# Exact block of ones for the bonus from the sixth unit on, and v weight conversions and two preparations issued behind masks and states

## Chip, cores and metric

The kernel runs on one core of a Trainium2 chip, as one program. The metric is the device time of one execution in microseconds (us). TensorE (PE; its weight loads are listed as PEld), VectorE (DVE), ScalarE (ACT), GpSimd (POOL) and SyncE (SP) work beside each other; each takes its instructions in the order in which they stand in the program, and waits for another engine or for a transfer by semaphores. SP issues most transfers, ACT some.

## The reference, cut to what matters

Three layers follow each other: a linear attention with a decaying state, a gated feed-forward layer, and a gated layer that mixes over the sequence.

```
B, H, S, D = 2, 8, 768, 48
for t in range(S):
    cur = einsum('bhd,bhe->bhde', u * k[t], v[t])
    y[t] = einsum('bhd,bhde->bhe', r[t], state + cur)
    state = w[t][..., None] * state + einsum('bhd,bhe->bhde', k[t], v[t])
...
xk = mu_k * x + (1 - mu_k) * x_prev;  xr = mu_r * x + (1 - mu_r) * x_prev
k = maximum(xk @ w_k, 0);  v = (k * k) @ w_v;  r = sigmoid(xr @ w_r);  x = r * v
...
h = gelu(x @ w_in);  u, v = split(h);  v = norm(v) * g
x = x + (u * (w_sg @ v + b_sg)) @ w_out
```

The term with `u` is the bonus: `y[t]` gets `v[t]` times the sum over d of `r[t] * u * k[t]`, a number for each token and head. The inputs are f32.

## The kernel before

The tokens are cut into four groups of 384 (two batches by two halves). The attention of one group is done for four pairs of heads, so there are 16 units of work, numbered here from 0 as in the code: unit g is head pair g % 4 of group g // 4. Each unit holds three chunks of 128 tokens. Units 0 to 3 run at the start, where little else is there to do. From then on the three matrix products of the first feed-forward layer of one group (keys "k", "r", "v") fill TensorE while the four units of the next group are put in between them. Units 4 to 7 thus stand among the feed-forward steps of group 0. The order of TensorE's instructions is written out by hand (`plan`, a list of keys with estimated times, and the loop over `keys` from L1068 on). The order of DVE, ACT, POOL and SP comes from a scheduler with a priority for each instruction (`with at(t)`) and with explicit "issue this behind that" constraints (`tc.issue_after`).

A unit has these steps:

- Preparation, `attn_prep` (L444), on DVE: a running product of the decay (`pf`), its reciprocal, a reversed scan (`pr`), then the scaled `kp` and `rp`. `prep(i)` issues all of it for unit i and first the loads of unit i + 1; `scans(i)` and `products(i)` issue it in two halves.
- `rk_make` (L477), on POOL: `ru`, the product of r and k for the bonus. It is issued behind the first DVE instruction on the scores of the unit before.
- "S", `attn_sc` (L482): on PE the transposes of `kp` (tile `kt_ps`), then what the bonus needs, then the scores `sc`; on DVE the two masked score blocks `am` (L546).
- "K", `attn_kv` (L553): on PE the states `kv`; on DVE the sums `zt`, on ACT the scaled blocks `sblk`.
- "Y", `attn_y` (L603), and "Z", `attn_z` (L618): the output `y` on PE from masked scores, bonus and states (`scar`, `sblk`), its copy to `yo`, and transfers from `yo` to `xx`, the input of the feed-forward layer.

The bonus has two forms. Below `U_DIAG` it is: three products of `ru` with a two-column matrix on PE (L495), then `vb` on DVE (L528), the values scaled by these sums, and six products of `vb` with the identity on PE (L615). From unit `U_DIAG` on (`wide(i)`) it is: `ru` times u is split into two halves by ACT (`rh`, L535) and DVE (`rh`, L537), two products with a block of ones `hblk` on PE give `ab` (L509, L510), and DVE multiplies `ab` with the transposed values `uvt` (L517), which SP loads for these units alone. DVE, not ACT, then adds the result to `y` (L636). `ab` and the `kv` of the same unit lie in one PSUM buffer, so that DVE must have read `ab` before PE can write `kv`. POOL's `ru` of the unit after is issued behind L517.

The weights come as raw 64-bit words. `load64` (L302) issues the load on SP and converts on ACT (`top`, L327) and DVE (L329), by way of two `top` buffers in turn. `conv_moe1` (L379) does this for the 8 blocks of `w_k`, 3 of `w_r`, 8 of `w_v`. The conversions of `w_v` (`wv`) have priorities that put them around units 5 and 6.

Of the kernel before, what the change touches and what calls it, by code (L numbers as in the profile page):

```python
# [24 lines left out]
NP = H // 2  # L25
# [25 lines left out]
T_GAP = 2.5  # L51
T_TAIL = 9.0
VQ = 4
U_DIAG = 6
L_SPLIT = 2
L_CV = 12
L_CVV = 8
L_CK = 6
# [14 lines left out]
def emit(tc, tin, nin, vt, consts, ucp, pars, b_sg, w_k, w_v, w_r, w_in, w_sgT, w_out, outT):  # L73
# [46 lines left out]
    split_ops = [True]  # L120
# [120 lines left out]
    def wide(i):  # L241
        return i >= U_DIAG

# [3 lines left out]
    def load_uvt(i):  # L247
        src = tin[subs[i // NP][0] * NP + i % NP]
        for q in rows(i == U_DIAG):
            with at(TS["Y", i] - (20 if i == U_DIAG else 9)):  # L250
                SP.dma_start(uvts[q], src[q, WL + 2 * G:WL + 3 * G])

    def load_t(i):
# [8 lines left out]
        for q in rows(i < 3):  # L262
            with at(TS["S", min(i, NP - 1)] - 8.5 if 2 <= i <= NP else TS["S", i] - L_UN + 0.5 if i > NP else -19.8 + 0.1 * i), after_table(i in (0,)):
                e.dma_start(rk[q], src[q, WL:WL + 2 * G].rearrange("p (q t) -> p q t", q=2))
        if i == U_DIAG:
            load_uvt(i)
# [17 lines left out]
    wt = {}  # L284
# [14 lines left out]
    def klpair(dt):  # L299
        return pl["w"].tile([128, 2 * WT + 2], dt, name="kl", tag="kl", bufs=KF // 2)  # L300

    def load64(full, src, dl, lc=L_CV):  # L302

        ld = dl - 7
        n_ = early["n"]
        if n_ < N_EARLY:
            stg = pair()
        elif N_EARLY + B_STG <= n_ < N_EARLY + B_STG + KF // 2:
            stg = klpair(U32)
        else:  # L310
            stg = pl["s"].tile([128, 2 * WT + 2], U32, name="stg", tag="stg", bufs=B_STG)
        if n_ < N_EARLY + B_STG + KF // 2:
            ld = T_EARLY + n_ * D_EARLY
        early["n"] += 1
        with at(ld):
            SP.dma_start(stg.bitcast(U16)[:, 1:1 + 4 * WT], src.bitcast(U16))
        n = full.shape[1]

        def box(x):
            return x.rearrange("p (c f) -> p c f", c=n)  # L320

        mid = box(stg[:, 1:1 + 2 * WT].rearrange("p (f w) -> p f w", w=2)[:, :, 0])
        end = box(stg.bitcast(BF16)[:, 4:4 + 4 * WT].rearrange("p (f w) -> p f w", w=4)[:, :, 0])
        top = tops["t"][tops["n"] % B_TOP]
        tops["n"] += 1
        with at(dl - lc - 1):
            A.activation(box(top.bitcast(F16).rearrange("p (f w) -> p f w", w=2)[:, :, 1]), end, AF.Copy)  # L327
        with at(dl - lc):
            V.scalar_tensor_tensor(full.bitcast(U32), mid, 13, box(top), ALU.logical_shift_right, ALU.bitwise_or)  # L329
# [18 lines left out]
    def split_lo(n, behind_):  # L348
        with tc.issue_after(behind_):
            for f in lows[:n]:  # L350
                f()
        del lows[:n]
# [26 lines left out]
    def conv_moe1(first=0, last=2 * KF + KM):  # L379
        def one(nm, i, src, dl):  # L380
            full1(nm, i, [128, KM, 128] if nm != "v" else [128, 1, DM])
            load64(wt[nm, i][0], src[i], dl, {"k": L_CK, "r": L_CV, "v": L_CVV}[nm])
            if NAT[nm] == 0 or (nm == "v" and i >= NVN):
                split1(nm, i, dl - (3 if nm == "v" else 0))

        todo = [("k", f, w_k, TS["k", 0, f]) for f in range(KF)]
        todo += [("r", f, w_r, TS["r", 0, f]) for f in range(KM)]
        todo += [("v", f, w_v, TS["v", 0, 0] + MM[0, "v"] * f) for f in range(KF)]
        for x in todo[first:last]:
            one(*x)  # L390
# [49 lines left out]
    st = {}  # L440
# [584 lines left out]
    def prep(i):  # L1025
        if i < NU:
            if i + 1 < NU and i >= 1:
                load_unit(i + 1)
            for _ in attn_prep(i):
                pass  # L1030
# [37 lines left out]
    for n, key in enumerate(keys[:n_in]):  # L1068
        kd, g = key[0], key[1]
# [50 lines left out]
        if kd == "K":  # L1120
            for f in head.pop("kl", []):
                with tc.issue_after(st[g + 1]["last"][1] if g + 1 in st else st[g]["zt"]), tc.issue_after(st[g]["sb"]):
                    f()
        if kd == "K" and g == 2 * NP - 2:
            with tc.issue_after(st[g]["zt"]), tc.issue_after(st[g]["sa"]):
                for f in range(LO_EARLY):
                    split1("k", f, TS["k", 1, f] - 12, V)
# [4 lines left out]
        if kd == "Z" and g == 2 * NP - 2:  # L1132
            scans(2 * NP)
        elif kd == "Z" and g == 2 * NP - 1:
            with tc.issue_after(st[g]["ev"]):
                products(2 * NP)
                scans(2 * NP + 1)
        elif kd == "Z" and g == 3 * NP - 1:
            with tc.issue_after(st[g]["zt"]):
                scans(g + 1)  # L1140
                products(g + 1)
                scans(g + 2)
        elif kd == "Z" and g == 3 * NP - 2:
            pass
        elif kd == "Z" and NP <= g < 2 * NP:
            prep(g + 2)
        elif kd == "Z" and g >= NP and g + 2 < NU:
            with tc.issue_after(st[g]["zt"]):
                scans(g + 2)
        if kd == "Z" and g >= NP:  # L1150
            if g % NP == NP - 1:
                if g // NP == 1:
# [5 lines left out]
                    a, v = mr[1]()  # L1158
# [5 lines left out]
        if kd == "S":  # L1164
            head["unit"] = g
            if g == LO_LAST:
                split_lo(NVN, st[g]["am"])
            if "sq" in head:
                with behind():
                    head.pop("sq")()  # L1170
# [92 lines left out]
```

## Time and profile before

| | |
|---|---|
| time, median of 3 runs | 335.16 us (335.05 to 335.48) |
| profiled execution, own time | 335.18 us |
| its span, first to last instruction | 333.3 us |
| granted TensorE clock, mean | 0.998 of full speed |
| PE busy | 325.5 us (98%) |
| DVE busy | 239.5 us (72%) |
| ACT busy | 187.1 us (56%) |
| POOL busy | 37.3 us (11%) |
| DVE busy in 45 to 56 us, 66 to 77 us | 9.26, 9.81 us of 11 |

The own time is 1.9 us over the span, what lies around the first and the last instruction. A busy share is taken over the whole span; what an engine has free in one stretch, such as the two in the last row, is read from that stretch. Matmul ends are modelled, so starts of PE instructions are the better guide.

### The profile page before, as it was taken

To read this page: it belongs to the slowest core of one execution; us is meant where nothing else is said; L and a number is where in the kernel's file an instruction comes from. 1 tells how busy PE (TensorE), PEld (TensorE's weight loads), DVE (VectorE), ACT (ScalarE), POOL (GpSimd) and SP (SyncE) were. 2 spreads that over 40 slices of the span, in tenths; PEclk is the share of its full clock that TensorE was granted. 3 is DMA by queue.
4 is the path that set the end of the run, shared out by engine and by line. 5 is a ranking of instruction groups with operands and counts; after the bars stand their busy time and mean duration, and the time that the engine had idled before them with its cause. 6 is when DMAs were issued, how large, how long until landed. Compare 5 with 4: busy or idle time off the path is not lost.

```text
span 333.3 us, 5954 instructions
## 1 busy us (share of the span) xinstructions
PE 325.5 (98%) x2139; PEld 286.2 (86%) x2139; DVE 239.5 (72%) x537; ACT 187.1 (56%) x447; POOL 37.3 (11%) x60
## 2 busy tenths in 40 slices
PE   7999999999999999999999999999999999999993
PEld 3786666666898999999999998998999999999993
DVE  5987998699699995998368451796989724555531
ACT  3566986759688645976369964954533215211100
POOL 3211102010111102011032540000000000000000
PEclk9999999999999999999999999999999999999999
DMA  8879963753524424011036126314140010100022
GB/s 216 213 236 314 289 211 99 207 118 104 177 81 107 111 74 121 16 39 36 24 109 185 53 71 211 94 41 97 49 98 7 1 71 2 63 10 0 0 76 79
DMA packets 23878, 34.22 MB, mean 103 GB/s; under 512 B 3440, under 2 KB 18160, under 8 KB 23840
## 3 DMA queue, kind: packets, MB, share of 16 engines
q1 hardware_dynamic: 21696, 31.34, 32.6%
q10 hardware_dynamic: 2144, 2.41, 2.8%
q8 instruction: 19, 0.31, 0.4%
q14 instruction: 19, 0.16, 0.2%
HBM read 29.02 MB, written 2.36 MB: 94 GB/s over the span
## 4 chain that ended last, share of the span: by engine, by line
PE 90%; ACT 3%; DMA 3%; DVE 1%; issue 1%; SPq 1%; ACTq 0%; DVEq 0%
PE mm L673 46%; PE mn L673 28%; PE sc L514 4%; PE y L612 3%; PE y L626 3%; PE kv L566 2%; DMA cst<-consts 2%; DMA wh<-w_r 1%; PE kt_ps L490 1%; ACT top L327 1%; PE y L615 1%; PE mm L495 1%; ACT sblk L592 1%; DVE pf L458 1%; PE ab L509 1%
## 5 line engine op out<-in xcount | busy, mean ns | idle before, releaser
L661 ACT ACTIVATE gah<-gt 128x384 fp32r<-128x384 f32 x16 | 8.4, 526 | 43.3 <-DVE gt L871 43.3
L480 POOL TENSOR_TENSOR ru<-urk 112x384 f32<-112x384 f32 x15 | 17.3, 1155 | 107.3 <-DVE ru L517 76.6
L592 ACT ACTIVATE sblk<-zt,pf 48x48 f32<-48x48 f32 x62 | 20.5, 330 | 7.6 <-DVE zt L576 4.2
L673 PE MATMUL mm<-kh,wh 128*128 128x384 f32 x64 | 22.0, 344 | 0.0
L673 PE MATMUL mm<-kh,wvl 128*128 128x384 f32 x64 | 21.6, 337 | 0.0
L673 PE MATMUL mm<-kl,wh 128*128 128x384 f32 x64 | 21.5, 337 | 0.0
L673 PE MATMUL mm<-xkh,wh 128*128 128x384 f32 x57 | 20.6, 361 | 0.0
L673 PE MATMUL mn<-wsh,vl 128*128 128x384 f32 x60 | 20.0, 334 | 0.0
L673 PE MATMUL mn<-wsh,vh 128*128 128x384 f32 x60 | 20.0, 334 | 0.0
L673 PE MATMUL mn<-wsl,vh 128*128 128x384 f32 x60 | 20.0, 334 | 0.0
L673 PE MATMUL mm<-xkl,wh 128*128 128x384 f32 x57 | 19.3, 338 | 0.0
L673 PE MATMUL mm<-xkh,wkl 128*128 128x384 f32 x57 | 19.2, 337 | 0.0
L776 DVE TENSOR_TENSOR kl<-kr,kh 128x384 fp32r<-128x384 f32 x24 | 14.1, 600 | 5.5 <-ACT kr L775 5.4
L458 DVE TENSOR_TENSOR_SCAN pf<-uw,d1f 112x387 f32<-112x387 f32 x16 | 16.0, 1005 | 2.4 <-DMA uw<-tin 2.4
L546 DVE TENSOR_TENSOR am<-sc,cst 128x384 f32<-128x384 f32 x32 | 16.1, 545 | 1.3 <-PE sc L514 1.3
L673 PE MATMUL mm<-xkh,wk 128*128 128x384 f32 x48 | 17.0, 497 | 0.0
L334 POOL TENSOR_TENSOR w2l<-wf,w2h 128x384 fp32r<-128x384 f32 x12 | 13.0, 1095 | 35.3 <-ACT w2h L333 35.3
L673 PE MATMUL mm<-kh,wv 128*128 128x384 f32 x48 | 16.3, 490 | 0.0
L327 ACT ACTIVATE top<-stg 128x384 f16<-128x384 bf16 x17 | 10.9, 642 | 8.4 <-DMA stg<-w_in 3.1
L463 DVE TENSOR_TENSOR_SCAN pr<-uw,d1r 112x387 f32<-112x387 f32 x16 | 15.3, 959 | 0.2
L707 ACT ACTIVATE dx<-xx,par 128x384 f32<-128x384 f32 x22 | 12.9, 607 | 4.1 <-DMA xx<-yo 4.0
L514 PE MATMUL sc<-rp,kp 48*128 48x128 f32 x192 | 15.0, 289 | 0.0
(223 smaller groups left out, 976.2 us busy)
## 6 DMA issues: line engine op xcount, KB each, us to landing
urk<-tin SPq DMA_DIRECT2D x26, 144.0 KB, 2.9
wh<-w_k SPq DMA_DIRECT2D x8, 384.0 KB, 5.4
stg<-w_in SPq DMA_DIRECT2D x8, 384.0 KB, 3.6
wq<-tin SPq DMA_DIRECT2D x16, 168.0 KB, 2.4
wsf<-w_sgT SPq DMA_DIRECT2D x12, 192.0 KB, 4.4
outT<-ot SPq DMA_DIRECT2D x12, 192.0 KB, 1.9
uv<-nin ACTq DMA_DIRECT2D x14, 144.0 KB, 3.3
uw<-tin SPq DMA_DIRECT2D x26, 72.8 KB, 2.6
```

The source lines that it names most:

```text
L327: A.activation(box(top.bitcast(F16).rearrange("p (f w) -> p f w", w=2)[:, :, 1]), end, AF.Copy)
L334: e.tensor_tensor(lo, full, hi.bitcast(F32), ALU.subtract)
L458: V.tensor_tensor_scan(pf[:, 0:n1], w[:, 0:n1], d1f[:, 0:n1], 1.0, ALU.mult, ALU.max)
L463: V.tensor_tensor_scan(pr[:, 1:wl][:, ::-1], w[:, 1:wl][:, ::-1], dr[:, 1:wl][:, ::-1], 0.0, ALU.mult, ALU.add)
L480: return e.tensor_tensor(rks[i], urk[i][:, 0], urk[i][:, 1], ALU.mult).ins
L514: PE.matmul(sc[h][:, c], s["kp"][hs, c], s["rp"][hs, c], start=True, stop=True)
L546: s["am"] = V.tensor_tensor(am[:, h], sc[h], mask, ALU.mult).ins
L592: s["sa"] = A.activation(sb[hs, hs], o[hs], AF.Copy, scale=s["pe"][c][hs]).ins
L612: PE.matmul(y3[hs, c], uv[i][:, c, h * D:PW if h else HP], s["at"][:, h, c], start=(c == 0), stop=False, skip_group_check=True)
L673: PE.matmul(ps, l, r, start=(first and k == 0), stop=(last and k == len(prods) - 1))
L707: ins = [A.activation(d, xj[:, 1 + t0:1 + t1], AF.Copy, scale=mu[:, j:j + 1]).ins]
L776: V.tensor_tensor(kl, kr, kh.bitcast(F32), ALU.subtract)
```

## The change

`U_DIAG` falls from 6 to 5, so that unit 5, the sixth, takes the second form of the bonus. The eight conversions of `w_v` are no longer issued with their loads: they are kept in a list, and three are issued at "S" of unit 5 behind its masks (`am`) and its transposed keys (`ka`), the other five at "K" of unit 5 behind its states (`zt`) and their scaled blocks (`sa`). The preparations issued by `prep(g + 2)` at "Z" of a unit stand behind that unit's `zt`. The branch is reached for units 4 and 5 alone, since units 6 and 7 are taken by the two branches above it; so the preparations of units 6 and 7 are moved, and those of 8 and 9, which `scans` and `products` issue, are not.

```diff
-U_DIAG = 6
+U_DIAG = 5
...
+    late = []
+
-    def load64(full, src, dl, lc=L_CV):
+    def load64(full, src, dl, lc=L_CV, later=False):
...
+        def conv():
+            to_f32(full, stg, box, dl, lc)
+
+        if later:
+            late.append(conv)
+        else:
+            conv()
+
+    def to_f32(full, stg, box, dl, lc):
         mid = box(stg[:, 1:1 + 2 * WT].rearrange("p (f w) -> p f w", w=2)[:, :, 0])
...
-            load64(wt[nm, i][0], src[i], dl, {"k": L_CK, "r": L_CV, "v": L_CVV}[nm])
+            load64(wt[nm, i][0], src[i], dl, {"k": L_CK, "r": L_CV, "v": L_CVV}[nm], nm == "v" and split_ops[0])
...
+        if kd == "K" and g == NP + 1:
+            with tc.issue_after(st[g]["zt"]), tc.issue_after(st[g]["sa"]):
+                for f in late[3:]:
+                    f()
...
         elif kd == "Z" and NP <= g < 2 * NP:
-            prep(g + 2)
+            with tc.issue_after(st[g]["zt"]):
+                prep(g + 2)
...
+            if g == NP + 1:
+                with tc.issue_after(st[g]["am"]), tc.issue_after(st[g]["ka"]):
+                    for f in late[:3]:
+                        f()
```

On DVE, between the bonus and masks of unit 5 and the scaled keys of unit 6 (`kp` from buffer `urk_108`), these rows stand before; `wv` are the conversions, `zt` the states of unit 5, `pf`, `d1r` and `pr` the preparation of unit 6:

```order
L528 TENSOR_TENSOR vb<-uv,kt_ps 128x288
L546 TENSOR_TENSOR am<-sc,cst 128x384 x2
L329 SCALAR_TENSOR_TENSOR wv<-kl,top_129 128x384
L329 SCALAR_TENSOR_TENSOR wv<-kl,top_128 128x384
L329 SCALAR_TENSOR_TENSOR wv<-kl,top_129 128x384
L329 SCALAR_TENSOR_TENSOR wv<-kl,top_128 128x384
L578 SCALAR_TENSOR_TENSOR zt<-zcar,kv 112x48
L458 SCALAR_TENSOR_TENSOR pf<-uw_105,d1f 112x387
L578 SCALAR_TENSOR_TENSOR zt<-zt,pf,kv 112x48
L460 RECIPROCAL d1r<-pf 112x3
L463 SCALAR_TENSOR_TENSOR pr<-uw_105,d1r 112x387
L467 TENSOR_TENSOR kp<-urk_108,pr 112x384
```

In the changed kernel the same stretch of DVE reads as follows (its lines are 11 further down):

```order
L557 TENSOR_TENSOR am<-sc,cst 128x384 x2
L340 SCALAR_TENSOR_TENSOR wv<-stg,top_129 128x384
L340 SCALAR_TENSOR_TENSOR wv<-stg,top_128 128x384
L340 SCALAR_TENSOR_TENSOR wv<-kl,top_129 128x384
L589 SCALAR_TENSOR_TENSOR zt<-zcar,kv 112x48
L589 SCALAR_TENSOR_TENSOR zt<-zt,pf,kv 112x48
L469 SCALAR_TENSOR_TENSOR pf<-uw_105,d1f 112x387
L471 RECIPROCAL d1r<-pf 112x3
L474 SCALAR_TENSOR_TENSOR pr<-uw_105,d1r 112x387
L340 SCALAR_TENSOR_TENSOR wv<-kl,top_128 128x384
L340 SCALAR_TENSOR_TENSOR wv<-kl,top_129 128x384
L478 TENSOR_TENSOR kp<-urk_108,pr 112x384
```

Six conversions were done ahead of the states of unit 5, and are three now; two more stand between `pr` and `kp` of unit 6, and the scan `pf` of unit 6 has both states ahead of it.

On DVE around the masks of unit 7, with `yo` and `ru` of units 6 and 7 and `wkl`, the low parts of split weights, these rows stand before:

```order
L713 TENSOR_TENSOR xkl<-dx,xkh 128x384
L329 SCALAR_TENSOR_TENSOR wv<-stg,top_129 128x384
L329 SCALAR_TENSOR_TENSOR wv<-stg,top_128 128x384
L368 TENSOR_TENSOR wkl<-wk,wh 128x384 x2
L636 TENSOR_TENSOR yo<-y,ru 112x384
L517 TENSOR_TENSOR ru<-ab,uvt 112x384
L368 TENSOR_TENSOR wkl<-wk,wh 128x384
L546 TENSOR_TENSOR am<-sc,cst 128x384 x2
L368 TENSOR_TENSOR wkl<-wk,wh 128x384
L458 SCALAR_TENSOR_TENSOR pf<-uw_107,d1f 112x387
```

In the changed kernel they read:

```order
L724 TENSOR_TENSOR xkl<-dx,xkh 128x384
L340 SCALAR_TENSOR_TENSOR wv<-stg,top_129 128x384
L340 SCALAR_TENSOR_TENSOR wv<-stg,top_128 128x384
L647 TENSOR_TENSOR yo<-y,ru 112x384
L528 TENSOR_TENSOR ru<-ab,uvt 112x384
L379 TENSOR_TENSOR wkl<-wk,wh 128x384
L557 TENSOR_TENSOR am<-sc,cst 128x384 x2
L379 TENSOR_TENSOR wkl<-wk,wh 128x384 x3
L469 SCALAR_TENSOR_TENSOR pf<-uw_107,d1f 112x387
```

Two of the `wkl` went from ahead of the masks to behind them. The ACT instructions that the last of the two conversions waits for stand before as follows, from `rh`, the first half for the bonus of unit 7, to the last `top`:

```order
L535 ACTIVATE rh<-ru,cst 112x384
L707 ACTIVATE dx<-xx_78,par 128x384
L786 ACTIVATE rs<-mm 128x384
L712 ACTIVATE xkh<-dx 128x384
L592 ACTIVATE sblk_86<-zt,pf 48x48 x2
L592 ACTIVATE sblk_87<-zt,pf 48x48 x2
L372 ACTIVATE wh<-wk 128x384
L327 ACTIVATE top_129<-stg 128x384
L372 ACTIVATE wh<-wk 128x384
L786 ACTIVATE rs<-mm 128x384
L327 ACTIVATE top_128<-stg 128x384
```

In the changed kernel they read:

```order
L546 ACTIVATE rh<-ru,cst 112x384
L797 ACTIVATE rs<-mm 128x384
L723 ACTIVATE xkh<-dx 128x384
L603 ACTIVATE sblk_86<-zt,pf 48x48 x2
L603 ACTIVATE sblk_87<-zt,pf 48x48 x2
L338 ACTIVATE top_129<-stg 128x384
L383 ACTIVATE wh<-wk 128x384 x2
L797 ACTIVATE rs<-mm 128x384
L383 ACTIVATE wh<-wk 128x384 x2
L338 ACTIVATE top_128<-stg 128x384
```

`dx` went ahead of `rh`, and two more `wh` stand ahead of the last `top`.

## Rows read from the trace of the kernel before

**Rows 1.** Chain of waits in order of time: start us, us, what.

```profile
44.70 0.34 ACT sblk L592
...
45.09 0.47 PE y L626 x2
...
327.84 0.56 DVE ot L881
```

**Rows 2.** Timeline of PE, units 5 and 6: start us, us, engine, line, operation.

```profile
45.39 0.45 PE L490 MATMUL kt_ps<-cst,kp 112*128 112x112 f32 x3
...
46.35 0.94 PE L514 MATMUL sc<-rp,kp 48*128 48x128 f32 x12
...
51.51 0.88 PE L612 MATMUL y<-am,uv 128*48 128x128 f32 x12
...
52.98 2.20 PE L673 MATMUL mm<-xkh,wk 128*128 128x384 f32 x6
...
55.67 0.45 PE L490 MATMUL kt_ps<-cst,kp 112*128 112x112 f32 x3
...
56.41 0.94 PE L514 MATMUL sc<-rp,kp 48*128 48x128 f32 x12
...
61.57 0.88 PE L612 MATMUL y<-am,uv 128*48 128x128 f32 x12
62.38 2.20 PE L673 MATMUL mm<-xrh,wr 128*128 128x384 f32 x6
```

**Rows 3.** Timeline of DVE, states of unit 5 and preparation of unit 6.

```profile
51.94 0.25 DVE L578 SCALAR_TENSOR_TENSOR zt<-zcar,kv 112x48 f32<-112x48 f32 x1
52.12 0.95 DVE L458 TENSOR_TENSOR_SCAN pf<-uw,d1f 112x387 f32<-112x387 f32 x1
...
53.35 0.96 DVE L463 TENSOR_TENSOR_SCAN pr<-uw,d1r 112x387 f32<-112x387 f32 x1
54.35 0.56 DVE L467 TENSOR_TENSOR kp<-urk,pr 112x384 f32<-112x384 f32 x1
...
55.29 0.61 DVE L537 SCALAR_TENSOR_TENSOR rh<-ru,cst,rh 112x384 fp32r<-112x384 f32 x1
```

**Rows 4.** Timeline of ACT: two conversions, a half for the bonus, two splits.

```profile
47.53 1.12 ACT L327 ACTIVATE top<-kl 128x384 f16<-128x384 bf16 x2
...
53.96 0.61 ACT L535 ACTIVATE rh<-ru,cst 112x384 fp32r<-112x384 f32 x1
...
66.09 0.92 ACT L372 ACTIVATE wh<-wk 128x384 fp32r<-128x384 f32 x2
```

**Rows 5.** SP's waits (total, times, longest us), timeline, transfers (KB, median us to landing).

```profile
SPq L264 <- DMA uv<-nin: 6.3, 1, 6.3
...
46.97 0.78 SPq L264 DMA_DIRECT2D urk<-tin  x2
...
urk<-tin SPq DMA_DIRECT2D x26, 144.0 KB, 2.9
```

**Rows 6.** Timeline of POOL and DVE: `ru` of units 5 and 7, scan of unit 5.

```profile
39.72 1.01 POOL L480 TENSOR_TENSOR ru<-urk 112x384 f32<-112x384 f32 x1 [4.18 <-DMA urk<-tin]
39.78 1.76 DVE L458 TENSOR_TENSOR_SCAN pf<-uw,d1f 112x387 f32<-112x387 f32 x1
...
57.21 1.54 POOL L480 TENSOR_TENSOR ru<-urk 112x384 f32<-112x384 f32 x1 [5.60 <-DVE ru L517]
```

**Rows 7.** Timelines of DVE and PE from unit 7 to the "k" products of group 1.

```profile
69.08 1.01 DVE L546 TENSOR_TENSOR am<-sc,cst 128x384 f32<-128x384 f32 x2
70.96 0.88 PE L612 MATMUL y<-am,uv 128*48 128x128 f32 x12
...
77.78 0.55 DVE L636 TENSOR_TENSOR yo<-y,ru 112x384 f32<-112x384 f32 x1
...
84.88 0.55 DVE L713 TENSOR_TENSOR xkl<-dx,xkh 128x384 fp32r<-128x384 f32 x1
85.49 0.45 PE L673 MATMUL mm<-xkl,wh 128*128 128x384 f32 x1
```

## The prediction

> **What bounds the kernel now.** I read the chain of waits first. Its last piece that is not PE work is a wait for ACT's `sblk` of unit 4, which ends at 45.04 us; from 45.09 on the chain is PE, piece after piece, to the last output at 327.84 [rows 1]. The reader is to see two things in that. What is taken off PE after 45 us comes off the end, and a PE wait put in after 45 us is added to the end, since nothing behind it is slack. The edit lies at 45 to 85 us, so I then read the timelines of PE, DVE and ACT there, and the order of the changed program.
>
> **What PE saves.** With the sums (unit 5) PE goes from `kt_ps` at 45.39 to `sc` at 46.35, 0.96 us; with the block of ones (unit 6) from 55.67 to 56.41, 0.74 us. From the first `y` product to the next `mm` it is 51.51 to 52.98, 1.47 us, in unit 5 with the six products of `vb`, and 61.57 to 62.38, 0.81 us, in unit 6 without them [rows 2]. So 0.22 + 0.66 = **0.88 us less**, if all that PE needs is there in time. Removing `vb` from DVE and the copy `yo` from ACT, both off the path, is worth nothing by itself: PE covers them.
>
> **What unit 5 must now wait for.** The second form needs two halves of `ru`. ACT is in `sblk` until 45.04 [rows 1]; its half takes 0.61 us [rows 4], so to 45.66. DVE's half starts on ACT's and takes 0.61 us [rows 3], so to 46.31. PE can then do the second of the two products at about 46.36 and `sc` 0.27 us later (an estimate, a good third of the 0.74 from `kt_ps` to `sc` in unit 6), at 46.63, where 46.35 - 0.22 = 46.13 was to be had: 0.50 us of wait. Unit 5 leaves **-0.38 us** (-0.88 + 0.50). DVE's multiplication L517 and the masks follow at 46.7 to 48.6, three conversions to 50.3, all before the states at 52.2: covered by PE's twelve `mm`. On SP one load of `uvt` is added and the last places in the queue turn: the wait of 6.3 us for a `uv` transfer, which held the first `urk` load of unit 6 until 46.97, falls to the second half of the `uw` load, and `urk` goes at 47.4 and 47.8. With the 2.9 us that `urk` takes, for the half as large `uw` too, they land at 49.9 and 50.7 [rows 5]; both are needed after 51, so I take nothing.
>
> **What unit 6 must wait for.** This is the first large term. The states of unit 5 come at 51.94 now, 0.43 after the first `y` product [rows 2, 3], and will come at 51.79 + 0.43 = 52.2, since unit 5's `sc` is 0.28 later than before. Both `zt` then stand ahead of the scan `pf`, which starts at about 52.65 (52.12 before). `pr` follows 1.2 us later, at 53.85, and `kp` would follow 1.0 us after that, at 54.85 [rows 3]. But two conversions stand between, and they need the `top` of ACT, which come behind the four `sblk` of unit 5. ACT's `sblk` take 0.34 each [rows 1] and follow `zt` at 52.5, with the k copies between, to about 54.0; two `top` take 1.12 [rows 4]: 54.0 to 55.1. The second conversion can start at 55.2, `kp` 0.47 later at 55.66, and DVE's half `rh` two slots of 0.47 after `kp` (54.35 to 55.29 [rows 3]), at 56.60, done at 57.21. PE, 0.38 us ahead, wants `kp` at 55.29 and that half 0.4 us later. It gets `kp` at 56.25 and does `sc` at 57.52, not at 56.41 [rows 2]. Unit 6's scores thus start **1.11 us later than before**; the 0.88 us are gone. Without the two conversions `rh` would be done at 56.4 and `sc` start at 56.7, +0.3.
>
> **What follows in units 6 and 7.** DVE stands 1.3 us behind (`rh` at 56.60, not 55.29). It goes on with `yo`, a conversion, `pf`, two masks, the reciprocal, `pr`, `rp`, `kp`, and only then L517 of unit 6, which before followed `rh` at once. With slots of 0.47 and 0.9 (scans) that is 61.9 to 62.45. PE needs it for `kv` of unit 6, since `ab` lies in that buffer, at 61.35 + 1.11 = 62.46: just in time. But POOL's `ru` of unit 7 waits for L517 too. It started at 57.21 [rows 6], and starts at 62.5 now. It took 1.01 to 1.54 us [rows 6]; I take 1.1, as DVE does little beside it. ACT's half for unit 7 is then done at 64.25. In ACT's queue stand behind it `rs`, `xkh`, four `sblk`, `top`, two `wh`, `rs`, two `wh` and the last `top`: with 0.34 for a `sblk`, 0.46 for a `wh` (0.92 for two), and 0.4 to 0.6 for each of the others [rows 1, 4] that is 5.3 us, to 69.6. The last conversion follows at 69.62, and `yo`, L517, a `wkl` and the two masks of unit 7, five slots of 0.47 and the last in full, to 72.5. PE comes to `y` of unit 7 at 70.96 + 1.11 = 72.07 [rows 7] and waits 0.45 for the second mask: **+1.54**.
>
> **What reaches the "k" products of group 1.** Before, DVE came from the masks of unit 7 (69.08) to its `yo` (77.78) in 8.70 us [rows 7], of which some 1.2 were waits for ACT. From the last conversion, 69.62, to `yo` the changed order has the same instructions and six more slots (the conversion, `yo`, L517, three `wkl` where one stood less the masks' own), 2.8 us: 81.1 if every wait stays, 80.7 with the handshakes followed one by one. That is 2.9 to 3.4 later. From `yo` a transfer, ACT's and DVE's `dx` and `xkl` lead to the product that PE had at 85.49, where it already waited for `xkl` of 84.88 [rows 7]. These instructions are the same in both orders, so this product is 2.9 to 3.4 us later too; I take 3.0. PE, 1.54 behind, waits 1.5 us more there. After it, PE has the work that it had, and the preparation of unit 8 is done: I see no later term.
>
> **The sum.** -0.88 + 0.50 + 1.49 (from -0.38 to +1.11) + 0.43 + 1.46 = **+3.0 us**. The span goes from 333.3 to 336.3, the time from the profiled execution's own 335.18 (0.02 over the median) to **338.2 us**. The least certain terms: POOL's `ru` of unit 7 (1.0 to 1.54, so -0.1 to +0.4), the ACT queue up to the last `top` (0.5 either way), the handshakes behind it (up to +0.4). Bounds of this case: 337.4 to 339.0.
>
> **A rule against it.** The scan of unit 5 took 1.76 us, not 0.95, while POOL's `ru` ran from 39.72 to 40.73 [rows 3, 6]: the two held each other up by 0.8 us. The Trainium skill (SBUF — State Buffer, "Who interferes with whom") says that a VectorE instruction with two SBUF inputs and a GpSimd instruction that reads SBUF exclude each other for a whole instruction. The trace agrees nearly: 0.8 of the 1.01 us were lost; a meeting of that kind would add 0.8 to the sum by the row, 1.0 by the rule. In my sum no scan meets `ru`: unit 6's `ru` is at 51.0 to 52.0, its scan at 52.65. Were `urk` 0.7 us late, the scan would be held, and everything from unit 6 on with it.
>
> **Rivals.**
> - *The later links hold.* If ACT's queue is 0.5 us quicker and the DVE waits between 70 and 78 us shrink as DVE falls behind, units 7 and 8 find what they need and only unit 6's wait stays: 335.18 + 1.1 = 336.3 us. For it: in my sum DVE stands still for ACT for some 3 us between 63 and 69 us. Against it: each of these instructions is behind another that is late.
> - *Port.* The scan of unit 6, or `dx` beside unit 7's `ru`, is held for 0.8 to 1.0 us: 339.1 us.
> - *Faster: the conversions do not delay `kp` of unit 6.* From the states at 52.2 DVE has until 55.3 for `kp` and until 55.7 for the end of `rh`, if PE is not to wait; without the two conversions `rh` would end at 56.4. It decides whether `zt` to the end of `rh` takes under 3.5 us; by the rows it takes 4.2 even without the conversions. If it did, -0.38 would stay: 334.8 us, and 334.3 if unit 5 did not wait either. Against it stand rows of DVE that are read off directly.
> - *No net change.* The saving stays in part and unit 6's wait is under 1 us: about 335.2 us. Part of the change does not do what its words say (units 8 and 9 are not moved), but what is moved is on the path.
>
> **How the numbers follow.** A run here varies by 0.43 us; 0.2% is 0.67 us, about what a measurement can tell. Chances: the forecast 0.55, the later links hold 0.20, port 0.08, faster 0.10, no net change 0.07. Slower by over 0.2%: 0.55 + 0.20 + 0.08 = 0.83; within it 0.07; faster 0.10. The range leaves out the faster case, the lower part of "no net change" and the upper part of the port case: 335.4 to 339.3 us.
>
> **What would show it.** In the trace after: `ab` and no `vb` in unit 5, and 0.4 us less from unit 5's `kt_ps` to unit 6's turn; unit 6's `kt_ps` waiting for DVE's `kp`, with two `wv` between `pr` and `kp` on DVE; `sc` of unit 6 near 57.5; POOL's `ru` of unit 7 near 62.5; the last `top` near 69; a PE wait at `y` of unit 7; the `xkl` product of group 1 near 88.5. I am wrong if `kp` of unit 6 ends before 55.5, or if PE has caught up with the old times at 88 us.

## The result and the profile after

The changed kernel takes **338.25 us** (338.02 to 338.30, 4 runs) against 335.32 us (335.05 to 335.48) of the kernel before on the same chip, a ratio of 1.0087 with a 95% interval of 1.0069 to 1.0104. The prediction was 338.2. The profiled execution took 338.21 us, its span is 336.3 us (333.3 before).

The page's busy time of each engine, and the chain that ended last by engine:

```profile
PE 325.9 (97%) x2123; PEld 285.4 (85%) x2123; DVE 240.2 (71%) x539; ACT 187.5 (56%) x447; POOL 37.4 (11%) x60
...
PE 79%; DVE 7%; ACT 6%; DMA 4%; issue 2%; SPq 1%; POOL 0%; ACTq 0%; DVEq 0%
```

PE executes 16 instructions fewer than before, and its printed busy time is 0.4 us longer (325.5 before) where the span is 3.0 us longer: the change adds no work to PE, it adds waits. A wait in the middle of a group of products is printed as busy. The chain, which before was PE from 45.09 us on [rows 1], now goes through DVE, ACT and POOL as well.

The timeline of PE over units 5 to 7 and the "k" products of group 1 (start us, us, engine, line, operation, and in brackets the idle time before it with what ended it; lines are 11 further down than before) answers to [rows 2, 7]:

```profile
45.49 0.45 PE L501 MATMUL kt_ps<-cst,kp 112*128 112x112 f32 x3
...
46.48 0.43 PE L521 MATMUL ab<-rh,hblk 112*112 112x384 f32 x1 [0.22 <-DVE rh L548]
46.84 0.94 PE L525 MATMUL sc<-rp,kp 48*128 48x128 f32 x12
...
51.99 0.88 PE L623 MATMUL y<-am,uv 128*48 128x128 f32 x12
52.80 2.20 PE L684 MATMUL mm<-xkh,wk 128*128 128x384 f32 x6
...
56.55 0.48 PE L501 MATMUL kt_ps<-cst,kp 112*128 112x112 f32 x3 [0.88 <-DVE kp L478]
...
57.45 0.43 PE L521 MATMUL ab<-rh,hblk 112*112 112x384 f32 x1 [0.25 <-DVE rh L548]
57.81 0.94 PE L525 MATMUL sc<-rp,kp 48*128 48x128 f32 x12
...
62.74 0.43 PE L577 MATMUL kv<-uv,kt 128*64 128x48 f32 x8
...
72.41 1.26 PE L623 MATMUL y<-am,uv 128*64 128x128 f32 x12
...
87.59 0.44 PE L684 MATMUL mm<-xkh,wh 128*128 128x384 f32 x1 [0.41 <-ACT xkh L723]
88.50 0.45 PE L684 MATMUL mm<-xkl,wh 128*128 128x384 f32 x1 [0.47 <-DVE xkl L724]
```

Four places are to be seen. Unit 5 has `ab` and no `vb`, and waits for DVE's half before the second of its two `ab` products. Unit 6 waits for `kp` and again for its half; `sc` comes at 57.81, where it was at 56.41. The `y` of unit 7 is 1.26 us long and not 0.88: inside the group the later products wait for the second mask. The `xkl` product of group 1 starts at 88.50 instead of 85.49. Behind it the shift against before stays at 3.02 us to the last product.

DVE between the states of unit 5 and the bonus of unit 6, then at the masks of unit 7 and ahead of the "k" products of group 1, answers to [rows 3, 7]:

```profile
52.26 0.27 DVE L589 SCALAR_TENSOR_TENSOR zt<-zcar,kv 112x48 f32<-112x48 f32 x1 [1.70 <-PE kv L577]
...
52.74 0.96 DVE L469 TENSOR_TENSOR_SCAN pf<-uw,d1f 112x387 f32<-112x387 f32 x1
...
53.95 0.96 DVE L474 TENSOR_TENSOR_SCAN pr<-uw,d1r 112x387 f32<-112x387 f32 x1
54.89 1.04 DVE L340 SCALAR_TENSOR_TENSOR wv<-kl,top 128x384 uint32<-128x384 uint32 x2
55.85 0.55 DVE L478 TENSOR_TENSOR kp<-urk,pr 112x384 f32<-112x384 f32 x1
...
56.78 0.61 DVE L548 SCALAR_TENSOR_TENSOR rh<-ru,cst,rh 112x384 fp32r<-112x384 f32 x1
...
62.03 0.55 DVE L528 TENSOR_TENSOR ru<-ab,uvt 112x384 f32<-112x384 f32 x1
...
69.87 0.56 DVE L340 SCALAR_TENSOR_TENSOR wv<-stg,top 128x384 uint32<-128x384 uint32 x1 [1.94 <-ACT top L338]
...
71.75 1.02 DVE L557 TENSOR_TENSOR am<-sc,cst 128x384 f32<-128x384 f32 x2
...
80.79 0.55 DVE L647 TENSOR_TENSOR yo<-y,ru 112x384 f32<-112x384 f32 x1
...
87.89 0.55 DVE L724 TENSOR_TENSOR xkl<-dx,xkh 128x384 fp32r<-128x384 f32 x1
```

POOL's `ru` of unit 7, then ACT from its half for unit 7 to the last `top`, the answer to [rows 4, 6]:

```profile
62.66 1.31 POOL L491 TENSOR_TENSOR ru<-urk 112x384 f32<-112x384 f32 x1 [10.52 <-DVE ru L528]
64.00 0.62 ACT L546 ACTIVATE rh<-ru,cst 112x384 fp32r<-112x384 f32 x1 [2.10 <-POOL ru L491]
...
68.39 0.93 ACT L383 ACTIVATE wh<-wk 128x384 fp32r<-128x384 f32 x2
69.22 0.62 ACT L338 ACTIVATE top<-stg 128x384 f16<-128x384 bf16 x1
```

This is the second chain: the bonus multiplication (L528 now, L517 before) of unit 6 ends at 62.58, POOL's `ru` starts on it, ACT's half on `ru`, the last `top` is the thirteenth instruction behind that half in ACT's queue, DVE stands still for it for 1.94 us ahead of the last `wv`, and the masks stand behind that `wv`.

### The profile page after: what moved, and what is told of

Same layout as the page of the kernel before. It is cut to its first block, busy times and chain, and to the rows that moved or that the text cites. A ratio compares the mean times of both kernels' runs of the same rounds, so it can differ in the third digit from the quotient of the medians.

```text
span 336.3 us, 5924 instructions
## 1 busy us (share of the span) xinstructions
PE 325.9 (97%) x2123; PEld 285.4 (85%) x2123; DVE 240.2 (71%) x539; ACT 187.5 (56%) x447; POOL 37.4 (11%) x60
## 4 chain that ended last, share of the span: by engine, by line
PE 79%; DVE 7%; ACT 6%; DMA 4%; issue 2%; SPq 1%; POOL 0%; ACTq 0%; DVEq 0%
PE mm L684 38%; PE mn L684 28%; PE sc L525 3%; PE y L623 2%; PE y L637 2%; DMA cst<-consts 2%; PE kv L577 2%; DVE pf L469 1%; ACT sblk L603 1%; ACT top L338 1%; DMA uv<-nin 1%; DVE wkl L379 1%; PE kt_ps L501 1%; DMA stg<-w_r 1%; ACT wh L383 1%
## 5 line engine op out<-in xcount | busy, mean ns | idle before, releaser
L684 PE MATMUL mm<-xkl,wh 128*128 128x384 f32 x57 | 19.3, 338 | 0.5 <-DVE xkl L724 0.5
L762 ACT ACTIVATE kr<-mm 128x384 f32<-128x384 f32 x27 | 12.7, 478 | 4.2 <-PE mm L684 3.5
```

The source lines that it names most:

```text
L684: PE.matmul(ps, l, r, start=(first and k == 0), stop=(last and k == len(prods) - 1))
L762: m1[s, "ev", f] = A.activation(kr, ps, AF.Relu).ins
```

## The experiments

The kernel before was run beside each and had medians of 335.3 to 335.4 us; e1 to e8 ran on one chip, e9 to e11 on another. What tells the kernels apart best is by how much the first transpose `kt_ps` of a unit starts later than in the kernel before (45.39, 55.67, 66.36 and 86.99 us for units 5 to 8). Unit 4 lies ahead of every edit; its column is how much the execution as a whole was off, and is to be taken from the others. The shifts come from one profiled execution of each kernel, the medians from all of its runs, so the two need not agree to better than some tenths of a us. Behind unit 8 the shift of PE no longer changes.

| kernel | median us (range, runs) | ratio, 95% | unit 4 | 5 | 6 | 7 | 8 |
|---|---|---|---|---|---|---|---|
| the change | 338.25 | 1.0069 to 1.0104 | +0.09 | +0.10 | +0.87 | +1.40 | +3.02 |
| e1_ones_only | 337.9 (337.4 to 339.45, 6) | 1.0068 to 1.0102 | +0.12 | +0.13 | +0.50 | +1.49 | +2.43 |
| e2_conv_only | 336.12 (335.82 to 336.48, 10) | 1.001 to 1.0032 | +0.06 | -0.04 | -0.04 | +0.92 | +0.92 |
| e3_ru7_early | 339.01 (338.14 to 339.71, 5) | 1.0092 to 1.0121 | -0.06 | -0.19 | +0.59 | +2.81 | +3.15 |
| e4_first_link | 338.32 (337.46 to 339.46, 6) | 1.0067 to 1.0103 | -0.21 | -0.20 | -0.47 | +0.52 | +2.45 |
| e5_ru7_again | 338.35 (338.16 to 339.14, 4) | 1.008 to 1.011 | +0.03 | -0.08 | +0.69 | +2.47 | +2.85 |
| e6_top_ahead | 337.81 (337.45 to 338.72, 6) | 1.006 to 1.0087 | -0.13 | -0.27 | +0.52 | +2.73 | +2.50 |
| e7_second_link | 338.74 (338.37 to 338.95, 4) | 1.0082 to 1.0112 | -0.03 | -0.03 | +1.07 | +3.22 | +3.22 |
| e8_both_links | 336.3 (335.76 to 338.45, 9) | 1.0015 to 1.0049 | -0.07 | -0.18 | -0.45 | +0.45 | +0.46 |
| e9_L517_early | 337.5 (336.26 to 338.25, 6) | 1.0043 to 1.0081 | +0.04 | -0.07 | +1.00 | +1.52 | +1.28 |
| e10_ones_mended | 336.29 (335.92 to 337.3, 10) | 1.0014 to 1.0036 | +1.31 | +1.19 | +1.08 | +1.61 | +1.93 |
| e11_all_mended | 334.85 (334.58 to 335.97, 12) | 0.9979 to 0.9998 | -0.08 | -0.22 | -1.09 | -0.94 | -0.66 |

The forecast times of e1, e2, e6, e10 and e11 were met to 0.4 us. The other six came out 0.8 to 2.5 us above what was forecast for a clock that does not fall; what was missed is said at each.

**The parts alone.** e1 is the block of ones for unit 5 without the moved conversions, e2 the moved conversions without it. In both, `prep` is called as before; that part by itself leaves the order of every engine as it was.

```diff
-            load64(wt[nm, i][0], src[i], dl, {"k": L_CK, "r": L_CV, "v": L_CVV}[nm], nm == "v" and split_ops[0])
+            load64(wt[nm, i][0], src[i], dl, {"k": L_CK, "r": L_CV, "v": L_CVV}[nm])
...
```

> The block of ones in unit 5 alone; the v conversions stay where they were before. Theory (two links: two conversions ahead of unit 6's kp, then a late L517 of unit 6 that holds POOL's ru of unit 7 and through ACT's queue the last conversion and unit 7's masks): without the moved conversions unit 6's sc starts near 57.3 us (56.41 before, 57.81 after), because yo of unit 5 still stands ahead of rh; but L517 of unit 6 still stands behind kp and rp of unit 7, so POOL's ru of unit 7 starts near 62.2 (57.21 before, 62.66 after), and most of the loss stays: 337.5 us (336.8 to 338.2). Rival 1 (the moved conversions are the whole loss): 334.8 us or less, faster than before. Rival 2 (the block of ones by itself costs more on PE than it gives): the loss would already show at unit 5's first mm behind y, later than 52.98.

```diff
-U_DIAG = 5
+U_DIAG = 6
...
```

> The v conversions moved alone; unit 5 keeps its sums and vb. Theory: one conversion stands between pr and kp of unit 6 and one between rp and rh, so rh and sc of unit 6 come 1.0 us later (sc near 57.4); L517 of unit 6 follows rh nearly at once, so POOL's ru of unit 7 starts near 58.5 and the second link is not there: 336.3 us (335.8 to 336.8). Rival 1 (conversions are the whole loss): 338.2 us. Rival 2 (they cost nothing, PE has slack there): 335.3 us.

DVE of e1 in unit 6:

```profile
51.91 1.23 DVE L340 SCALAR_TENSOR_TENSOR wv<-kl,top 128x384 uint32<-128x384 uint32 x1 [0.33 <-ACT top L338]
53.06 0.25 DVE L589 SCALAR_TENSOR_TENSOR zt<-zcar,kv 112x48 f32<-112x48 f32 x1
...
56.41 0.55 DVE L647 TENSOR_TENSOR yo<-y,ru 112x384 f32<-112x384 f32 x1
56.88 0.60 DVE L548 SCALAR_TENSOR_TENSOR rh<-ru,cst,rh 112x384 fp32r<-112x384 f32 x1
```

DVE of e2 in unit 6:

```profile
54.43 0.56 DVE L340 SCALAR_TENSOR_TENSOR wv<-kl,top 128x384 uint32<-128x384 uint32 x1 [0.32 <-ACT top L338]
54.91 0.55 DVE L478 TENSOR_TENSOR kp<-urk,pr 112x384 f32<-112x384 f32 x1
...
55.84 0.55 DVE L340 SCALAR_TENSOR_TENSOR wv<-kl,top 128x384 uint32<-128x384 uint32 x1
56.31 0.61 DVE L548 SCALAR_TENSOR_TENSOR rh<-ru,cst,rh 112x384 fp32r<-112x384 f32 x1
57.44 0.56 DVE L528 TENSOR_TENSOR ru<-ab,uvt 112x384 f32<-112x384 f32 x1
```

Each part alone makes unit 6 late, by another way. In e1 a conversion beside POOL's `ru` takes 1.23 us, so the states come at 53.06, and `yo`, now an instruction of DVE, stands ahead of `rh`; `sc` starts at 57.90 (57.3 expected). In e2 two conversions stand ahead of `rh`, and `sc` starts at 57.33 (57.4 expected). The two do not add. At `sc` of unit 6 they cost 1.49 and 0.92 us alone and 1.40 together, since both are paid at the same wait, PE's for DVE's half `rh`. From unit 7 to unit 8 e1 loses 0.94 and e2 nothing, and the change loses 1.62, more than both. Of the two parts only e1 has the late L528 of unit 6 (61.34; in e2 it comes at 57.44, right behind `rh` as before); with the moved conversions as well it comes at 62.03 and the last `top` at 69.22 (67.98 in e1).

**The second chain.** e3 lets POOL's `ru` of unit 7 start behind the masks of unit 6, not behind L528. It was run twice, the second time as e5.

```diff
-            tc.add_manual_dep(rk_make(i + 1, PL), s["am0"].name, mybir.DependencyInfo(
+            tc.add_manual_dep(rk_make(i + 1, PL), s["am" if i == NP + 2 else "am0"].name, mybir.DependencyInfo(
```

> The changed kernel, with one wait changed: POOL's ru of unit 7 waits for unit 6's masks, which stand two slots and more ahead of L517, and not for L517. The first link stays: sc of unit 6 at 57.8 as after. Theory: ru of unit 7 starts near 60.2 and not at 62.66, ACT's rh of unit 7 near 61.5 and not at 64.00, the last top and the last conversion come 1.9 us earlier, unit 7's masks no longer hold PE, and the xkl of group 1 is ready when PE wants it: 336.5 us (336.2 to 337.2). Rival (PE's delay in unit 6 alone carries the loss on, and everything later is only late with it): 338.2 us, as after.

In its profile `ru` is at 59.92 and ACT's half at 60.95, as meant, and yet unit 7 is 2.81 us late. The windows of e3 (busy us of PE, PEld, DVE, ACT and POOL, granted TensorE clock, DMA share, GB/s) show another thing:

```profile
58.00:60.00 2.00, 2.00 (x13) 1.27 (x10) 1.97 (x6) 0.00 (x0) 0.08 (x1) 0.61 0.16 37
60.00:62.00 2.00, 2.00 (x5) 1.09 (x4) 2.00 (x2) 0.61 (x1) 0.92 (x1) 0.54 0.75 212
```

The granted clock is 0.61 and 0.54, near the lower level, and the twelve `mm` of that stretch take 5.83 us (4.14 in the profile of the change). That decides nothing about the chain.

> The same kernel as e3_ru7_early, because in that one's profile TensorE ran at a granted clock of 0.54 to 0.61 from 58 to 62 us, which took 1.7 us and hid what was asked: whether an earlier ru of unit 7 brings the last top, and all behind it, forward. Theory: where the clock stays at 1.00, the last top comes near 67.5 us (69.22 after), unit 7's masks near 70.4 (71.75), kt_ps of unit 8 1.7 us later than before (3.02 after): 337.0 us in the lower runs. Rival (the late ru only fills a gap, and rs and xkh would hold ACT anyway): last top near 69, kt_ps of unit 8 at +2.8 or more, 338.2 us.

This time the clock is 1.00 there. The timeline of e5, POOL and DVE, then PE, then ACT:

```profile
60.02 1.00 POOL L491 TENSOR_TENSOR ru<-urk 112x384 f32<-112x384 f32 x1 [7.42 <-DVE d1r L471]
60.06 1.77 DVE L474 TENSOR_TENSOR_SCAN pr<-uw,d1r 112x387 f32<-112x387 f32 x1
...
63.20 0.55 DVE L528 TENSOR_TENSOR ru<-ab,uvt 112x384 f32<-112x384 f32 x1
...
63.85 0.40 PE L577 MATMUL kv<-uv,kt 128*64 128x48 f32 x8 [1.21 <-ACT rs L797]
...
64.31 0.52 ACT L723 ACTIVATE xkh<-dx 128x384 fp32r<-128x384 f32 x1 [1.15 <-DVE dx L720]
...
68.64 0.63 ACT L338 ACTIVATE top<-stg 128x384 f16<-128x384 bf16 x1
```

The early `ru` holds the scan by 0.8 us and lets `rh` of unit 7 go ahead of L528, which comes 1.2 us later than in the change. `kv` of unit 6 lies in the buffer of `ab`, so PE waits 1.21 us there (the row names ACT's `rs`, a step that had ended 0.7 us before; L528 ends at 63.75, 0.10 before `kv`). And the last `top` hardly gains: it comes at 68.64 (67.5 expected, 69.22 in the change), since ACT's queue now stands at `xkh`, which needs DVE's `dx`, and `dx` stands behind L528 too. The masks come at 71.65 and the `xkl` of group 1 at 87.73, as good as in the change (71.75 and 87.89). So the rival was right (+2.85 at unit 8, 338.35 us): the early `ru` saves next to nothing, because ACT hangs on L528 in two ways, through `ru` and `rh` and through `dx` and `xkh`, and L528 itself came later. PE loses less from unit 7 to unit 8 than in the change (0.38 for 1.62) only because it has already lost 1.21 at `kv`.

e6 takes another member out of the chain: the last `top` ahead of the second pair of `wh` in ACT's queue. e7 is e3 and e6 together.

```diff
...
-                    split1("k", f, TS["k", 1, f] - 12, V)
+                    with tc.issue_after(head["top"]) if f > 1 else contextlib.nullcontext():
+                        split1("k", f, TS["k", 1, f] - 12, V)
```

> The changed kernel, with ACT's last top put ahead of the second pair of wh, where it stood before; POOL's ru of unit 7 still waits for L517. Theory (the second link is ACT's queue behind rh of unit 7, and two wh of 0.46 us belong to it): last top near 68.4 us, kt_ps of unit 8 0.5 us earlier than after, at +2.5: 337.7 us. Rival (the place of the last top is the whole second link): kt_ps of unit 8 at +1.5, 336.7 us.

> The changed kernel without its second link: ru of unit 7 behind unit 6's masks, and the last top ahead of the second pair of wh. The first link stays (sc of unit 6 near 57.8). Theory: last top near 66.6 us, masks of unit 7 in time for PE, the xkl of group 1 ready when PE wants it, so that kt_ps of units 7 and 8 are both 1.4 us later than before: 336.7 us. Rival (what DVE does between unit 7's masks and its yo is late for another reason): kt_ps of unit 7 at +1.4, of unit 8 still at +2.5 or more, 337.8 us or more. If the clock falls at 58 us as in e3, add 1.7.

e6 came out as expected in time (337.81), but the granted clock of its profile is 0.67 and 0.50 in 58 to 62 us, so its shifts hold two effects. Its last `top` came at 68.07 (68.4 expected), and PE, late by the clock, does not wait at `xkl`. e7 has 0.54 and 0.61 there, and its last `top` is as late as in the change:

```profile
69.19 0.64 ACT L338 ACTIVATE top<-stg 128x384 f16<-128x384 bf16 x1 [0.53 <-DMA stg<-w_v]
```

The forecast was 66.6. The `xkl` of group 1 is at 88.09 (87.89 in the change). From unit 7 to unit 8 e7 loses nothing more (+3.22 at both) only because PE, 1.8 us later at unit 7 than in the change, comes to that product about when DVE's `xkl` is done (88.65). So e7 does not show that its two edits end the second chain; its time of 338.74 is near the 338.4 forecast for a fall of the clock.

e9 changes the place of L528 itself: the preparation of unit 7 is issued in two pieces, its `pr`, `rp` and `kp` behind L528 of unit 6.

```diff
+        elif kd == "Z" and g == NP + 1:
+            load_unit(g + 3)
+            with tc.issue_after(st[g]["zt"]):
+                head["rest"] = attn_prep(g + 2)
+                next(head["rest"])
...
+            if g == NP + 2:
+                with tc.issue_after(st[g]["am0"]):
+                    for _ in head.pop("rest"):
+                        pass
```

> The changed kernel with one thing changed: pr, kp and rp of unit 7 stand behind L517 of unit 6, so that L517 comes some 1.8 us earlier on DVE (near 60.2 us, 62.03 after), and with it both what waits for it: POOL's ru of unit 7 and kv of unit 6 (whose buffer ab lies in; e5 showed that PE waits 1.2 us for it when L517 slips to 63.2). The first link stays: sc of unit 6 near 57.8. Theory: ru of unit 7 near 60.9, last top near 67.7 (69.22 after), no wait of PE at kv or at the masks of unit 7, the xkl of group 1 in time: kt_ps of units 7 and 8 both 1.4 us later than before, 336.7 us; 1.7 more in runs where the clock falls at 58 us. Rival (the late part is a matter of DVE's and ACT's load, not of L517's place): kt_ps of unit 8 at +2.5 or more, 337.8 us.

DVE, POOL and ACT of e9:

```profile
60.24 0.52 DVE L528 TENSOR_TENSOR ru<-ab,uvt 112x384 f32<-112x384 f32 x1
...
60.85 1.59 POOL L491 TENSOR_TENSOR ru<-urk 112x384 f32<-112x384 f32 x1 [6.53 <-DVE ru L528]
...
67.35 0.63 ACT L338 ACTIVATE top<-stg 128x384 f16<-128x384 bf16 x1
...
69.89 1.02 DVE L557 TENSOR_TENSOR am<-sc,cst 128x384 f32<-128x384 f32 x2
```

L528 is 1.8 us earlier, the last `top` 1.9, the masks of unit 7 1.9, and PE waits at none of `kv`, masks and `xkl`. The shift of unit 6 stays (+1.00), that of unit 8 falls from +3.02 to +1.28. The profiled execution took 336.43 us; the median is 337.5, with a granted clock of 0.993 to 0.996 in the four higher runs (1.000 and 0.997 in the two lower). The mechanism is shown by the profile; the 0.8 us more in the median are not explained. A fall of the clock as in e3, 1.69 us on twelve `mm`, would fit the higher runs, but none of them has a trace.

What ties the second chain to the time can be read across all thirteen profiles: the `xkl` of group 1 starts on DVE 18.4 to 19.3 us behind the last `top` on ACT, wherever that `top` lies between 64.89 us (e11) and 69.22 (the change).

**The first chain.** e4 issues the five late conversions behind the masks of unit 6 and puts the scan `pf` of unit 6 ahead of the states of unit 5.

```diff
...
-        if kd == "K" and g == NP + 1:
-            with tc.issue_after(st[g]["zt"]), tc.issue_after(st[g]["sa"]):
-                for f in late[3:]:
-                    f()
...
+                    with tc.issue_after(head["pf"]) if i == NP + 1 else contextlib.nullcontext():
+                        s["zt"] = V.scalar_tensor_tensor(o, z[0], z[1], kv3[:, c], ALU.mult, ALU.add).ins
...
+            if g == NP + 2:
+                with tc.issue_after(st[g]["am"]), tc.issue_after(st[g]["ka"]):
+                    for f in late[3:]:
+                        f()
```

> The changed kernel without its first link: the five late conversions go behind unit 6's masks and unit 6's scan pf goes ahead of the states of unit 5, so that nothing but pr stands between the states and kp. L517 of unit 6 stays behind kp and rp of unit 7. Theory: kp of unit 6 near 53.8 us, rh near 55.2, PE waits for neither and sc of unit 6 starts near 56.1 (56.41 before, 57.81 after); DVE gets to L517 of unit 6 near 60.6, POOL's ru of unit 7 starts near 61 and the second link costs about 1 us instead of 1.9: 335.8 us (335.0 to 336.6). Rival (the second link is all that counts from unit 7 on): 337.5 us or more, although sc of unit 6 is early.

`kp` is at 53.47 and `kt_ps` of unit 6 no longer waits (55.20), but `sc` starts at 56.93, not at 56.1. `yo` of unit 5 stands ahead of `rh` and waits for PE until 55.40, and ACT's half stands behind a `kr` until 55.26. The size was wrong: behind the conversions stood two more in the line for `rh`. The second chain takes another 1.9 us from unit 7 to unit 8, where about 1 was expected, and so the rival came out (337.5 us or more although `sc` is early): the last `top` is at 68.02, and what PE had won in unit 6 it waits for at the `xkl` product. The profiled execution also ends 1.1 us later behind its last product than the kernel before does, which no row explains.

e8 is e4, e3 and e6 together, with `yo` of unit 5 issued behind `rh` of unit 6 and ACT's half ahead of that `kr`.

```diff
...
+        if i == NP + 1:
+            head["yo"] = out
+        else:
+            out()
...
+            if g == NP + 2:
+                with tc.issue_after(st[g]["rl"]):
+                    head.pop("yo")()
...
+        if kd == "K" and g == NP + 1:
+            halves[g + 1] = bonus_hi(g + 1)
```

> The changed kernel without either link: v conversions behind unit 6's masks, unit 6's scan pf ahead of unit 5's states, ACT's half rh of unit 6 ahead of the k copy that waits for PE, yo of unit 5 behind DVE's half rh, ru of unit 7 behind unit 6's masks, the last top ahead of the second pair of wh. Theory: PE does not wait in unit 6 (sc near 56.1, 56.41 before), kt_ps of unit 7 at -0.3 and of unit 8 at -0.3 to +0.3 against before: 335.1 us (334.7 to 335.7), as fast as before or a little faster. Rival (the block of ones in unit 5 costs in itself what it saves, or something later is late for a reason that the two links don't hold): kt_ps of unit 8 at +1.0 or more, 336.3 us or more.

Now `sc` of unit 6 is at 56.15, as expected. It follows `kt_ps` by 0.92 us where 0.74 is without a wait, so 0.18 of the wait for the halves is left; the larger wait of PE in unit 6 is at `kv` (0.67 us, L528 ends at 61.73 and `kv` starts at 61.82). Unit 8 is at +0.46, between forecast and rival, and the profiled execution took 335.96 us; the median is 336.3, for 335.1 forecast.

e10 is e1 with the order mended as in e8 and L528 early as in e9, e11 is e8 with L528 early, right behind the masks of unit 6, and two edits for unit 5. In both POOL's `ru` of unit 7 waits for L528 again, without the edit of e3. The edits for unit 5 are ACT's half ahead of the `sblk` of unit 4, and one `w_r` conversion behind the masks.

```diff
...
+            if g == NP:
+                halves[g + 1] = bonus_hi(g + 1)
...
-                    for f in late[:3]:
+                    for f in late[:4]:
                         f()
```

> The block of ones in unit 5 with the mended order of e8 and with L517 early, but with the v conversions where they were before. Up to kt_ps of unit 6 it differs from e8 only in the conversions. Theory (the four conversions behind unit 5's masks reach to 53 us, since ACT has their top late, and push the states, pf, pr and kp of unit 6): kt_ps of unit 6 at +0.3 or more (e8: -0.45), sc near 57.2, kt_ps of unit 8 near +0.9: 336.2 us. Rival (with pf ahead of the states the conversions fit, as they did before the change): kt_ps of unit 6 at -0.4, and of unit 8 at -0.4: 334.9 us.

> e8 with three things more: L517 of unit 6 right behind unit 6's masks, so that kv of unit 6 does not wait for it (0.67 us in e8); in unit 5 ACT's half rh ahead of the states of unit 4, and the last w_r conversion behind unit 5's masks, so that PE does not wait for the halves of unit 5. Theory: kt_ps of unit 6 at -1.0 (e8: -0.45), sc near 55.5, kt_ps of unit 7 at -0.9; then the xkl of group 1, which DVE has near 84.5, takes some of it back: kt_ps of unit 8 at -0.5 (-0.9 to +0.1), 334.8 us (334.4 to 335.4), faster than before by less than can be measured well. Rival (the saving of 0.9 us on PE is not there at all): kt_ps of unit 6 at -0.3 or later, 335.3 us or more.

e10 came out as expected in its time, 336.29, and in part of its steps. In its profile the clock was 0.50 and 0.64 in 10 to 14 us, which shifts all from unit 1 on by 1.31 us. Less that, `kt_ps` of unit 6 is at -0.23, nearer to the rival (-0.4) than to the theory (+0.3), `sc` at 56.71 (57.2 expected) and unit 8 at +0.62 (+0.9). PE of e11 in units 5 and 6 and at the `xkl` product:

```profile
45.17 0.45 PE L501 MATMUL kt_ps<-cst,kp 112*128 112x112 f32 x3
...
45.92 0.94 PE L525 MATMUL sc<-rp,kp 48*128 48x128 f32 x12
...
54.58 0.45 PE L501 MATMUL kt_ps<-cst,kp 112*128 112x112 f32 x3
...
55.48 0.94 PE L525 MATMUL sc<-rp,kp 48*128 48x128 f32 x12
...
60.41 0.43 PE L584 MATMUL kv<-uv,kt 128*64 128x48 f32 x8
...
84.84 0.44 PE L699 MATMUL mm<-xkl,wh 128*128 128x384 f32 x1 [0.26 <-DVE xkl L739]
```

e11 has none of the waits up to unit 6 and gains 0.87 us from unit 5 to unit 6 (-0.22 to -1.09). Two small ones are left behind that: `sc` of unit 6 follows `kt_ps` by 0.90 us and not 0.74, and the `xkl` product waits 0.26 us. 334.85 us is 3.4 us under the change and 0.5 us under the kernel before, an interval that only just leaves out no change.

## Why the prediction was right

The time (338.25 for 338.2), the span (336.3 for 336.3) and the places of the loss came out as the sum had them. That the total fits to 0.05 us is in part luck: the last conversion came 0.25 us later than forecast (69.87 for 69.62), and its way to `yo` of unit 7 took 10.92 us where the sum had 11.1 to 11.5. The bounds beside the sum, 337.4 to 339.0, don't follow from the uncertainties named with them, which add up to 337.6 to 339.5; the measured time lies in both. Step by step:

- **What PE saves**, 0.88 us: e11, where PE does not wait, shows 0.87 from unit 5 to unit 6. Shown.
- **What unit 5 waits for**, +0.50: in the change `sc` starts 1.35 us behind `kt_ps`, and 0.74 without a wait [rows 2], so 0.61. The printed idle time of 0.22 is less, as it counts from the modelled end of the product before. With ACT's half moved ahead (e11) `sc` follows after 0.75: the wait was for the halves. Shown; the term was 0.1 short, nearly all of it because `sc` followed the second product by 0.36 and not by the estimated 0.27. The turn of SP's queue cost nothing, as taken: POOL's `ru` of unit 6 started on its `urk` at 51.15 (51.0).
- **Unit 6**, `sc` +1.11: measured +1.40. 0.09 of it is the whole execution (unit 4 is at +0.09 already), 0.11 the term before, 0.09 its own: `zt` 52.26, `kp` 55.85 and `rh` 56.78 were forecast at 52.2, 55.66 and 56.60. By the forecast's own slots (`kp` at 54.85 without the conversions, and two of 0.47) `kp` had to come at 55.79; the sum let the first conversion start before `pr` was done. That what stands ahead of `kp` and `rh` is the cause is shown by e2, e4 and e8 together: without the conversions between `pr` and `rh`, with `pf` and the half earlier, all but 0.18 us of the wait is gone. e4 adds what the sum did not see: with the conversions gone, `yo` of unit 5, now DVE's work, and ACT's place for its half hold `rh` next.
- **L517 of unit 6 just in time for `kv`**: it ends at 62.58, and `kv` starts at 62.74 without a wait. How near that was, e5 and e8 show: when L528 slips behind its need, PE stands 1.21 and 0.67 us.
- **The masks of unit 7**, +0.43: `y` starts at 72.41 and takes 1.26 for 0.88, so +0.38. POOL's `ru` started at 62.66 (62.5 forecast), the last `top` ended at 69.84 (69.6), the masks at 72.77 (72.5): all 0.2 to 0.3 later, as PE was. `ru` took 1.31 us and not 1.1; ACT's queue made up 0.1 of it.
- **The `xkl` product of group 1**, +1.46: 88.50 as forecast near 88.5; with PE already 1.45 + 0.38 = 1.83 late behind the masks, that is 1.18 more. This term was 0.28 too large because the ones before it were 0.29 too small: DVE sets the time of this product, so what PE loses on the way to it is not paid again. That the late L517 and ACT's queue behind it are the cause is shown by e9, which moves L517 alone and takes unit 8 from +3.02 to +1.28; the two terms were 1.89 together, and 1.74 went. That the way from L517 to the last `top` leads through POOL's `ru` holds for the change as it stands, where the rows meet end to start, but `ru` is not the only way: with `ru` freed, e5 had the last `top` held by `dx` behind L517.
- **The rivals.** That the later links would hold (336.3) is what e9 gives in its profiled execution, 336.43, with L528 moved up by hand; as written, ACT's queue from the half to the last `top` took 5.22 us against 5.3, no 0.5 us quicker. The port rival did not come: `pf` of unit 6 took 0.96, and `dx` beside `ru` of unit 7 took 0.61 (`ru` itself 1.31). In e1 and e5 such meetings do come. The faster rival hung on `zt` to the end of `rh` in under 3.5 us: it took 5.13 us (5.0 forecast).
- **The preparations behind `zt`**: no row of any engine changes place by them; the changed program is the same, instruction for instruction, with and without that edit. So they cost nothing, as taken. The scan `pf` of unit 6 stands behind both states only where the block of ones and the moved conversions come together: in e1 and in e2 it stands between them.

## What to carry to other kernels

When an instruction moves off the bound engine, count what stands ahead of its new prerequisites on the engines that take over: here PE gave up 0.88 us of work and got some 3.8 us of waits, because the half for the bonus and L517 stood behind other work on DVE. A wait that one engine pays early is not the end: follow each late instruction through every queue that starts on it until a step with slack, since PE paid twice more, some 15 and 30 us later. And mend such a chain at the late member that all the later ones hang on: freeing POOL's `ru` alone (e5) moved PE's wait to `kv` and left ACT waiting for L517 by another way, issuing L517 early (e9, e11) ended it.

## What the hardware showed that was not expected

- **Granted clock.** In the profiles of e3, e6 and e7 the granted TensorE clock falls to 0.50 to 0.67 in 58 to 62 us, near the 1.2 GHz level. In e3 and e6 twelve `mm` take 5.83 us in place of 4.14, in e7 they take 5.15 and the `sc` ahead of them 1.55 in place of 0.94; in e10 it falls in 10 to 14 us. The profiles of the change, of e5 (the kernel of e3) and of e9 have like waits of PE just before (0.88 to 1.18 us for `kp`, 0.89 to 1.20 in e3, e6 and e7) and keep 1.00. What decides it stays open; two executions of one kernel differ by it.
- **DVE and POOL hold each other.** `ru` alone takes 1.00 us; in e5 the scan beside it takes 1.77 and not 0.96, in e8 `ru` takes 2.10 between two DVE instructions, of which `kp` takes 1.36 and not 0.55 (rows below). The Trainium skill (SBUF — State Buffer, "Who interferes with whom") has it that a VectorE instruction with two SBUF inputs contends with a GpSimd instruction that reads SBUF, and that issue order decides which of them waits. These rows agree: in e5 0.81 us of the 1.00 of `ru` are lost by the scan that came second, in e8 first by `ru`, then by `kp`.
- **The named releaser.** For `kv` in e5 and e8 the trace names ACT (`rs`, `dx`), which was not the last to finish; the reader of the shared buffer, DVE's L528, ended 0.1 us before `kv` started in both.

POOL and DVE of e8, for the second point:

```profile
58.27 2.10 POOL L491 TENSOR_TENSOR ru<-urk 112x384 f32<-112x384 f32 x1 [5.29 <-DVE am L564]
...
59.43 1.36 DVE L478 TENSOR_TENSOR kp<-urk,pr 112x384 f32<-112x384 f32 x1
```
